# Forgetting attention and a bilinear feed-forward layer in one kernel: the last 64 queries as full tiles, value products as visits of their own, the last output in halves, and a new order

## The chip, the cores and the metric

The kernel runs on one core of a Trainium2 chip. The core has engines with a queue each, which run side by side and wait for one another through semaphores: TensorE (PE in the profile; its weight loads are PEld), VectorE (DVE), ScalarE (ACT), GpSimd (POOL) and SyncE (SP), which issues most of the DMA transfers. Every queue is worked off strictly in the order in which its instructions stand. The metric is the device time of one execution in microseconds (us).

## The reference, cut to what matters

There are 8 batches with 8 heads each, 576 positions and 64 dimensions per head. The attention has a decay from a running sum of log f; its output is the input of a bilinear layer.

```python
cum = np.cumsum(np.log(np.clip(f, 0.0001, 1.0)), axis=-1)
scores = scale * np.matmul(q, k.transpose(0, 1, 3, 2))
scores = np.where(causal, -1e9, scores + cum[:, :, :, None] - cum[:, :, None, :])
attn = exp(scores - max) / sum            # 576 x 576 per head
x = np.matmul(attn, v)                    # to 4608 tokens x 512
out = ((x @ w_a) * (x @ w_b)) @ w_out     # 512 -> 1536 -> 512
```

## The kernel before, in words

**Units of the attention.** A unit t is a pair of heads of one batch: t = 4 * batch + pair, 32 units in all. One head of the pair lies on partitions 0 to 63 of the tiles qT and kT, the other on partitions 64 to 127, so a score matmul contracts over 64 partitions only, and the matmuls of the two heads are issued one after the other for the two halves of the array. The 576 queries are four blocks of 128 (i = 0 to 3) and a last one of 64 (i = 4). `groups` (line 640) puts them in four groups: group 0 is the blocks 1 and 0, group 1 block 2, group 2 block 3, group 3 the last 64 queries. In group 3 the result of one head goes to partitions 0 to 63 and that of the other to 64 to 127, so its matmuls use 64 x 64 of the array each (`qk_group`, lines 413 to 429): two with 512 keys, two with 64 keys, and two that add the causal mask from `low` and `neg64`.

**What a unit goes through.** Score matmuls write a PSUM tile `sc`, of which there are two (RING, line 104); each group takes one. DVE adds the decay and takes the maximum (line 520 of `do_decay`), and writes S; that frees `sc`. ACT takes the exponential and its sum (551, and 547 for i = 4), DVE the reciprocal (561, 559), POOL multiplies by it (569). The blocks 0 to 2 make the tile PA, the blocks 3 and 4 the tile PB. SP issues a transposing DMA of each (`do_tr`, line 583; for batch 0 PE transposes instead). PE then multiplies with the values (`do_pv`, 611, and `do_pv4`, 627, for the last 64 queries), and DVE copies the result to xT (237 and 638).

**Visits of TensorE.** A scheduled piece of work is an `Op`; one for PE is called a visit here. For batches 0 and 1 (`EARLY`) the groups 0 and 1 are visits, and groups 2 and 3 are one. From batch 2 on (units 8 to 31, `MASKP`) there are two visits a unit: groups 0 and 1 together, and groups 2 and 3 together (line 693). The first of them also does the value products of unit t - 2 (LAG, line 656); their last 64 queries go to a spare corner of the group-0 tile of `sc`, so that tile is only free again when DVE has copied them out (`do_ev4`, 638).

**The feed-forward layer.** The 4608 tokens are cut into eleven chunks. For each of 12 feature blocks there are four matmuls for w_a (`psa`) and four for w_b (`psb`, line 888), ACT copies the first result, DVE multiplies the two (899); then three groups of four matmuls a block of 128 tokens make the output (`pso`, 908), which ACT and DVE copy out in turn (233, 237) and SP stores (918). A chunk can only start when all its tokens' attention is done. There are 372 such groups of four matmuls; they fill PE between the visits of the attention.

**The order.** All Ops are made in program order and numbered. A list of numbers, ORDER (line 990), then gives the order in which they are issued, and CHOICE (line 1092) says which engine an Op that could run on several takes. Nothing is scheduled on the chip: each engine runs its part of ORDER in that order. q, k and v of a batch come by SP's DMAs (244, 263), are cast to fp16 (235, 237) and q and k are transposed on PE (278); f comes by two DMAs (165); its running sum needs `clip`, a logarithm, `scan` and `low_part` (177 to 185). The weights come by POOL's DMAs (385), eight for w_a and w_b.

Of the kernel before, what the change touches and what calls it, by code (L numbers as in the profile page):

```python
# [25 lines left out]
def kernel(  # L26
# [11 lines left out]
    nc = tc.nc  # L38
# [23 lines left out]

    crow = perm.tile([128, S], FP16, tag="crow", name="crow")
# [25 lines left out]
    def paddings():  # L89
        for x in PB:  # L90
            nc.gpsimd.memset(x[:, 12, 64:128], 0.0)
        for i in range(2):
            nc.gpsimd.memset(nv[i][64:128, NSB - 1, :, :], 0.0)
# [12 lines left out]
            "sc": 2, "pv": 1, "ff": 3}  # L106
# [35 lines left out]
    def take(op, tag):  # L142

        users = [op]
        op.takes.append((tag, users))
        return users
# [257 lines left out]
    def qk_group(t, g):  # L404
# [6 lines left out]

        if g == 3:
# [232 lines left out]
    ev_ops, late, last_bc, last_pb = {}, {}, [], []  # L645
# [12 lines left out]
    def attention(t, base):  # L658
# [34 lines left out]
        for gs in ([(0,), (1,), (2, 3)] if b in EARLY else [(0, 1), (2, 3)]):  # L693
# [3 lines left out]
            old = None  # L697
            if gs == (0, 1) and (t - LAG) // NP not in EARLY and t >= LAG:
                old = t - LAG
# [8 lines left out]
            qk = Op("PE", dur * COLS * 1.06 + (0.08 if gs == (2, 3) else 0.0), stage, deps, prio=prio(gs[0]), mode="row", name=f"qk{t}.{gs[0]}")  # L708
            if old is not None:
                qk.durs = {"PE": dur * COLS * 1.06 + 0.1 + 10 * 128 * COLS * 1.05 + 0.15}  # L710
                qk.last = "col"
                qk.deps.extend(late[old][0])
            if qk_prev:
                qk.deps.append(qk_prev)
            qk_prev = qk
# [4 lines left out]
            if old is not None:  # L720
                late[old][1](qk, sc_of[0])
            for u in (kq_users[("q", b)], kq_users[("k", b)]):
                u.append(qk)
        direct_ex = {}
# [201 lines left out]
    def ffn(t0, n):  # L926
# [27 lines left out]
        for tb in range(n // 128):  # L954
            p = base + 12 + tb
            prev = []
            for part in range(3):
# [11 lines left out]
                prev = [mo]  # L969
            oc = Op(*(("DVE", 0.69) if tb % 2 else ("ACT", 0.59)), lambda e, tb=tb: ff_ocopy(e, t0, tb), prev, prio=-2000 + p, name="ocopy")  # L970
# [16 lines left out]
    for n in cuts:  # L987
# [3 lines left out]
        26 1 0 20 32 38 44 3 4 27 2 19 21 22 28 5 11 6 12 29 30 7 13 14 8 9 33 10 31 34 267 16 18 23-25 61 64  # L991
# [5 lines left out]
        235 108 236 249 85 250 95 90 127 1635-1637 1639 87 253 1641 128 1640 1638 133 1642 184 86 91 129 185 134  # L997
        130 1643 96 1644-1646 97 153 258 132 131 254 251 141 98 102 135 172 99 178 136 59 126 259 142 255 256
# [6 lines left out]
        342 1680 1681 343 1682 484 380 381 344 485 274 391 392 296 474 297 303 304 239 1683-1685 308 467 475  # L1005
        298-300 476 305 1686 324 486 1688 306 393 346 347 353 354 488 348 349 487 302 417 301 307 468 350 355
        1689 240 1690 1691 418 237 469 419 238 470 471 374 477 479 408 1693 1694 420 421 396 397 1695 1696
        411 412 356 403 1697-1700 352 337 395 351 330 394 480 357 338 310 1701 315 481 404 316 398 399 1702 483
        422 425 432 423 311 1703 426 400 1704 482 405 309 491 1687 493 360 358 1705 1706 427 433 406 312 439 440
        1707 1709 1711 435 1710 1708 1712 428 313 434 314 424 1713 442 1714 441 402 401 407 478 429 431 1715  # L1010
        1717 1718 446 447 1716 453 361 1719-1721 1723 454 443 533 448 1725 1722 449 1726 1727 496 345 494 1724
# [4 lines left out]
        547 554 414 532 531 461 462 556 1749 537 1751-1753 559 1754 1755 1757 1756 1759-1761 1758 560 1762 663  # L1016
        445 459 558 574 535 549 551 557 1763 1765 1764 542 1766 564 1767 1769 1768 1770 561 565 1771-1777 664
        543 544 658 550 1778 576 665 562 563 566-568 577 666 1779 1780 659 660 580 588 578 569 570 581 661 463
        1781 464 1783 465 1785 582 1784 1750 594 1782 587 1787 583 1788 590 1786 466 595 1789 1791 579 584 1790
        589 591 601 615 669 1745 670 592 571 572 667 683 674 1793 1795 1792 596 597 1794 598 1796 1797 602 1798  # L1020
        585 616 575 593 603 604 606 599 586 600 607 605 1799-1801 608 1802 671 609 618 610 1804-1806 619 622 630
        629 636 637 620 623 1807 624 672 632 673 611 612 668 684 675 1809 631 625 1810 639 638 681 613 614 725
        679 621 1811 1813-1815 643 1812 644 1817 617 640 633 1816 645 648 626 649 642 1819 1818 1820 646 647 627
        1821-1824 676 651 650 686 677 652 678 653 654 641 628 634 635 682 1825 1827 1829 690 1826 692 691 698
        704 1828 688 705 697 700 1831 1833 1830 693 706 1834 699 707 1835 1832 694 687 1836 701 689 856 656 655
        851 1803 1837-1839 711 708 712 1840 696 680 695 710 685 716 713 703 857 726 709 714 702 715 852 717
        1841-1843 1845 1844 1847 728 1849 1846 718 719 732 1848 720 1850 1851 1853 734 1854 722 721 730 739 733
        740 1852 1855 1856 746 747 1857 853 1858 1859 731 741 854 749 742 735 1860 858 748 859 860 729 855 863
        767 809 736 753 754 864 727 755 743 750 758 759 756 1862-1864 724 723 1808 1861 1867 770 1868 1869
        760 761 737 768 757 861 762 1865 745 763 764 774 788 776 790 751 738 752 789 791 792 782 772 775 781 794  # L1030
        744 1870 1872 1873 784 777 783 1874 1876 766 773 765 877 875 873 1877 1875 771 865 1878 866 867 1880
        1882 862 795 796 778 785 810 769 1879 800 797 801 1881 802-804 798 1883 786 793 780 799 787 779 805 806
# [107 lines left out]
```

## Time and profile before

| | us |
|---|---|
| median of 3 runs | 416.04 (415.64 to 416.44) |
| the profiled execution | 417.89 |
| its span, first to last instruction | 416.2 |
| PE busy | 390.6 (94%) |
| DVE / ACT / POOL busy | 302.3 / 278.1 / 255.0 |
| first matmul starts | 5.38 |
| mean granted TensorE clock | 0.995 |

The profile is of one execution, 1.85 us longer than the median of the runs shown. Busy times say how much of the span an engine worked; PE's ends are modelled, so two matmuls that run one behind the other overlap in these figures, and the distance from one start to the next is the better measure. A group's line gives its busy time, the mean duration of one instruction, then the idle time in front of it and what ended that. A timeline row gives start, time, engine and line, operation, tiles and shapes, the number of merged instructions, and in brackets the idle time in front.

### The profile page before, as it was taken

The numbers are of one execution on the slowest core, as the hardware profiler recorded it, in microseconds if no ns is written. First come the engines' busy times: TensorE is split into PE (matmuls) and PEld (weight loads), VectorE is DVE, ScalarE is ACT, GpSimd is POOL, SyncE is SP. The second block draws the span as 40 slices with busy tenths as digits, with TensorE's granted clock in tenths as the row PEclk, the third lists the DMA queues.
The fourth block names the chain that finished last, engine by engine and source line by source line (L and its number), as shares of the span: only waits on it lengthen the run. The fifth ranks groups of instructions, "written<-read, shape, count | busy, mean of one in ns | idle before, by whom it ended". The sixth has DMA issues, their size and how long they took to land. (4 is left out here: it accounts for less than half of the span.)

```text
span 416.2 us, 10946 instructions
## 1 busy us (share of the span) xinstructions
PE 390.6 (94%) x3860; PEld 212.1 (51%) x3860; DVE 302.3 (73%) x1006; ACT 278.1 (67%) x790; POOL 255.0 (61%) x439
## 2 busy tenths in 40 slices
PE   1789999799998999999999999999999999999996
PEld 1456766566655544444444544444454444444552
DVE  5998998697777778867877889688877885342240
ACT  5886997685777578786878778677787773231231
POOL 7999898469477867686685586766856655000000
PEclk9999999899999999999999999999999999999999
DMA  8999999999999999999999999999966738200202
GB/s 261 240 217 237 184 223 224 180 234 195 243 247 224 285 246 194 275 229 273 235 229 245 251 253 196 230 215 292 213 138 165 162 63 173 95 0 2 101 2 76
DMA packets 153432, 80.58 MB, mean 194 GB/s; under 512 B 130720, under 2 KB 133280, under 8 KB 153376
## 3 DMA queue, kind: packets, MB, share of 16 engines
q1 hardware_dynamic: 149616, 75.15, 79.3%
q0 software_dynamic: 3760, 4.72, 6.9%
q8 instruction: 30, 0.49, 0.5%
q14 instruction: 26, 0.21, 0.2%
HBM read 52.05 MB, written 9.58 MB: 148 GB/s over the span
## 5 line engine op out<-in xcount | busy, mean ns | idle before, releaser
L520 DVE CUSTOM_DVE_ANT_0 S<-sc,spread 64x576 f32<-64x576 f32 (+4 forms) x232 | 124.9, 562 | 10.6 <-ACT PA L551 3.1
L888 PE MATMUL psb<-xT,wb 128*128 128x512 f16 (+2 forms) x528 | 116.1, 343 | 0.4 <-ACT a L233 0.4
L888 PE MATMUL psa<-xT,wa 128*128 128x512 f16 (+2 forms) x528 | 115.8, 342 | 0.3
L899 DVE TENSOR_TENSOR ht<-psb,a 128x512 f16<-128x512 f32 (+2 forms) x132 | 77.4, 589 | 34.0 <-PE psb L888 30.6
L233 ACT CAST a<-psa 128x512 f16<-128x512 f32 (+2 forms) x132 | 66.2, 502 | 51.6 <-PE psa L888 43.5
L551 ACT ACTIVATE PA<-S,st 128x256 f16<-128x256 f32 (+2 forms) x168 | 84.1, 503 | 24.2 <-DVE st L520 22.6
L908 PE MATMUL pso<-wout,ht 128*128 128x512 f16 x432 | 98.5, 379 | 0.0
L569 POOL TENSOR_SCALAR PA<-PA,st 128x384 f16<-128x384 f16 (+2 forms) x192 | 89.8, 480 | 12.4 <-DVE st L561 11.0
L569 POOL TENSOR_SCALAR PB<-PB,st 128x512 f16<-128x512 f16 (+1 forms) x96 | 67.5, 712 | 30.1 <-DVE st L561 16.4
L888 PEld LDWEIGHTS <-wb 128*128 128x128 f16 x528 | 50.1, 98 | 41.3 <-issue 1.3
L888 PEld LDWEIGHTS <-wa 128*128 128x128 f16 x528 | 49.4, 98 | 40.8 <-issue 1.8
L908 PEld LDWEIGHTS <-ht 128*128 128x128 f16 x432 | 40.6, 98 | 46.7 <-issue 0.5
L551 ACT ACTIVATE PB<-S,st 128x512 f16<-128x512 f32 x56 | 40.1, 717 | 11.7 <-DVE st L520 7.7
L410 PE MATMUL sc<-kT,qT 64*128 64x256 f16 (+5 forms) x480 | 43.7, 277 | 3.3 <-ACT PA L551 1.5
L551 ACT ACTIVATION_READ_ACCUMULATOR PA<-S,st 128x1 f32 x168 | 31.9, 190 | 0.0
L561 DVE RECIPROCAL st<-st 128x2 f32<-128x2 f32 x128 | 18.5, 158 | 18.2 <-ACT PB L551 13.1
L410 PEld LDWEIGHTS <-qT 64*128 64x128 f16 (+1 forms) x480 | 17.0, 98 | 28.2 <-issue 18.5
L486 POOL TENSOR_SCALAR_AFFINE_SELECT spread<-spread 128x256 f32<-128x256 f32 x24 | 9.8, 408 | 35.1 <-DVE st L520 35.1
L237 DVE CAST xT<-pv 128x512 f16<-128x512 f32 (+1 forms) x40 | 23.0, 575 | 8.8 <-PE pv L611 8.6
L547 ACT ACTIVATE PB<-S,st 128x576 f16<-128x576 f32 x28 | 21.8, 777 | 9.9 <-issue 6.5
L233 ACT COPY osb<-pso 128x512 f32<-128x512 f32 x19 | 10.9, 575 | 24.3 <-DMA out_dram<-osb 12.8
L520 DVE CUSTOM_DVE_ANT_1 S<-sc,spread 128x256 f32<-128x256 f32 x48 | 19.6, 420 | 9.4 <-PE sc L627 4.7
(85 smaller groups left out, 427.6 us busy)
## 6 DMA issues: line engine op xcount, KB each, us to landing
spread<-cum_d SPq DMA_DIRECT2D x24, 576.0 KB, 5.6
out_dram<-osb SPq DMA_DIRECT2D x36, 256.0 KB, 3.0
q<-in_q_dram SPq DMA_DIRECT2D x15, 576.0 KB, 5.7
k<-in_k_dram SPq DMA_DIRECT2D x15, 576.0 KB, 5.5
v<-in_v_dram SPq DMA_DIRECT2D x32, 256.0 KB, 5.5
wout<-in_moe_w_out_dram POOLq DMA_DIRECT2D x3, 512.0 KB, 6.4
v<-in_v_dram SPq DMA_DIRECT2D x8, 128.0 KB, 4.9
wa<-in_moe_w_a_dram POOLq DMA_DIRECT2D x2, 512.0 KB, 8.6
```

Of the source, the lines that this page charges most:

```text
L233: nc.scalar.copy(out=out_, in_=in_)
L237: VEC[e].tensor_copy(out=out_, in_=in_)
L410: nc.tensor.matmul(out=dst, lhsT=lhsT, rhs=rhs, start=start, stop=stop, skip_group_check=True)
L486: nc.gpsimd.affine_select(out=x, in_=x, compare_op=mybir.AluOpType.is_ge, fill=NEGBIG, base=0, pattern=[[0, 2], [-1, 128]], channel_multip ...
L520: nc.vector.tensor_tensor_reduce(out=o, in0=x, in1=y, scale=-1.0, scalar=3e38, op0=ADD, op1=MIN, accum_out=m)
L547: nc.scalar.activation(out=p_blocks(t, 4), in_=T[("s" if direct else "z", t, 4)], func=EXP, bias=st[:, 8:9], scale=sign, accum_out=st[:, 1 ...
L551: nc.scalar.activation(out=p_blocks(t, i)[:, :, h, :], in_=(T[("s", t, i)][:, h, :] if direct else T[("z", t, i)][:, h * n:h * n + n]).rea ...
L561: nc.vector.reciprocal(out=st[:, 20 + 2 * i:22 + 2 * i], in_=st[:, 10 + 2 * i:12 + 2 * i])
L569: VEC[e].tensor_scalar(out=p, in0=p, scalar1=st[:, c:c + 1], scalar2=1.0, op0=MUL, op1=MUL)
L888: nc.tensor.matmul(out=p[:, 0:n], lhsT=w16[:, db, 128 * fb:128 * fb + 128], rhs=xTflat[db][:, t0:t0 + n], start=(db == 0), stop=(db == 3))
L899: nc.vector.tensor_tensor(out=ht[:, 0:n], in0=T.pop(("psb", t0, fb))[:, 0:n], in1=T.pop(("a16", t0, fb))[:, 0:n], op=MUL)
L908: nc.tensor.matmul(out=o, lhsT=T[("ht", t0, fb)][:, 128 * tb:128 * tb + 128], rhs=wout16[:, fb, :], start=(fb == 0), stop=(fb == 11))
```

## The change

Four things are changed.

1. From batch 2 on the scores of the last 64 queries (group 3) are made with 128 x 128 matmuls. POOL copies the two heads' 64 queries into a tile `qd` (two of them, zero elsewhere) whose two diagonal blocks are the two heads, so that one matmul gives both; three matmuls (512 keys, 64 keys, mask with the block-diagonal tile `lowd`) take the place of six. `paddings` clears `qd` and `lowd` at the start and fills `lowd`.
2. The visits of units 8 to 31 are one a group instead of one for two groups, and the value products of unit t - 2 are a visit of their own, `pv`, which may come any time after group 0 of unit t.
3. The last 128 tokens' output is copied in two halves, by DVE and ACT, and stored by two DMAs, from ACT's queue and SP's.
4. ORDER and CHOICE are replaced as a whole by another result of the search.

What the new order does can be read from the sequence of instructions on each engine. On PE the groups of a unit come as 0, 1, 3, 2 as a rule, and group 0 of unit t + 1 mostly stands right behind group 2 of unit t. SP issues the two loads of f ahead of the first loads of q and k; before, q came first. DVE casts the first q and k alone (before: q by DVE and ACT, k by POOL) and makes both low parts of the first 256 positions; POOL makes both of the rest, the first of them ahead of the second q's casts. Two of the w_b loads (512 KB each) stand on POOL behind the normalizations of block 2 and some of block 3 of batch 0. SP issues the first transpose of unit 5 ahead of its second one, of unit 6's second one and of two loads of the running sum. The 372 groups of feed-forward matmuls keep their own order.

```diff
+    qd = [perm.tile([128, 128], FP16, tag=f"qd{i}", name=f"qd{i}") for i in range(2)]
+    lowd = perm.tile([128, 128], FP16, tag="lowd", name="lowd")
...
     def paddings():
+        for x in (*qd, lowd):
+            nc.gpsimd.memset(x, 0.0)
+        for r in HP:
+            nc.gpsimd.tensor_copy(out=lowd[r, r], in_=low[0][r, 0:64])
...
+        if g == 3 and t in MASKP:
+            x = qd[t % 2]
+            mm(c[:, 0, :], x, kT[:, pr, 0:SF], start=True, stop=True)
+            mm(c[:, 1, 0:64], x, kT[:, pr, SF:S], start=True)
+            mm(c[:, 1, 0:64], lowd, neg64, stop=True)
+            T[("s", t, 4)] = c.rearrange("p a k -> p (a k)")[:, 0:S]
+            return
...
+    def last_queries(t):
+        b, pr = divmod(t, NP)
+        for r in HP:
+            nc.gpsimd.tensor_copy(out=qd[t % 2][r, r], in_=T[("T", "q", b)][r, pr, SF:S])
...
-        for gs in ([(0,), (1,), (2, 3)] if b in EARLY else [(0, 1), (2, 3)]):
+        for gs in ([(0,), (1,), (2, 3)] if b in EARLY else [(0,), (1,), (2,), (3,)]):
...
-            def stage(_, gs=gs, old=old):
+            def stage(_, gs=gs):
                 for g in gs:
                     qk_group(t, g)
-                if old is not None:
-                    do_pv(old, (0, 1, 2, 3), {"A", "B"})
-                    do_pv4(old, T.pop(("spare", t)))
...
+            if full:
+                cp = Op("POOL", 0.4, lambda _: last_queries(t), [kq_ops[("q", b, pr)], o_p] + last_qd[-1:], prio=prio(0),
+                        name=f"qd{t}")
...
+            old = t - LAG
+            if gs == (0,) and b not in EARLY and old // NP not in EARLY:
+                pv = Op("PE", 10 * 128 * COLS * 1.05 + 0.15,
+                        lambda _, old=old: (do_pv(old, (0, 1, 2, 3), {"A", "B"}), do_pv4(old, T.pop(("spare", t)))),
+                        [qk, *late[old][0]], prio=prio(0), mode="col", name=f"pv{old}")
+                sc_of[0].append(pv)
+                late[old][1](pv, sc_of[0])
...
+    def last_copy(e, t0, tb, part):
+        if ("osb", t0, tb) not in T:
+            T[("osb", t0, tb)] = osb_pool.tile([128, 512], FP32, tag="osb", name="osb")
+        c = slice(256 * part, 256 * part + 256)
+        cast(e, T[("osb", t0, tb)][:, c], T[("pso", t0, tb)][:, c], False)
+
+    def last_store(t0, tb, part):
+        r0, c = t0 + 128 * tb, slice(256 * part, 256 * part + 256)
+        (nc.sync if part else nc.scalar).dma_start(out=out[r0:r0 + 128, c], in_=T[("osb", t0, tb)][:, c])
...
+            if t0 + 128 * tb + 128 == NT:
+                ou = None
+                for part, (e, d) in enumerate((("DVE", 0.41), ("ACT", 0.39))):
...
     ORDER = """
-        26 1 0 20 32 38 44 3 4 27 2 19 21 22 28 5 11 6 12 29 30 7 13 14 8 9 33 10 31 34 267 16 18 23-25 61 64
...
+        0 1 26 20 32 38 3-6 27 28 11 7 2 29 30 12 21 22 8 10 9 13 14 19 33 34 23 24 31 25 18 61 64 35 70 106 15
...
     CHOICE = """
-        PDPPPPAADAADPDADAPDAPPPDDDDDAADDDDDDDDADAAADAADDDDDAAAAAAADADAAAADAAAAADDAAAAAAAAAAAAAADDAAAADAAADDA AAA
+        DDPPDDAADDADAPDAPPDDPPPDDAADDDADDDDADDAAAAAADADDADDDDAAAAADADAAAAAAAADADDADAAAAAAADAADADADAAAADADAAA AAA
```

More of the change, by code (lines that the diff above doesn't have):

```diff
@@ L105 @@
             "LA0": 1, "LA1": 1, "LA2": 1, "LA3": 1, "PA": 4, "PB": 2, "PTA": 3, "PTB": 2, "st": 6, "ht": 14, "a16": 3, "osb": 2,
-            "sc": 2, "pv": 1, "ff": 3}
+            "sc": 2, "qd": 2, "pv": 1, "ff": 3}
     SM = 3 * 128
@@ L644 @@
     MAXD = {0: 0.42, 1: 0.69, 2: 0.96, 3: 1.22, 4: 0.75}
-    ev_ops, late, last_bc, last_pb = {}, {}, [], []
+    ev_ops, late, last_bc, last_pb, last_qd = {}, {}, [], [], []
     first_of = {}
@@ L696, in attention @@
                       + (128 * len(groups[g]) * (t not in MASKP) if g < 3 else 128) for g in gs)
-            old = None
-            if gs == (0, 1) and (t - LAG) // NP not in EARLY and t >= LAG:
-                old = t - LAG
-            def stage(_, gs=gs, old=old):
+            full = gs == (3,)
+            def stage(_, gs=gs):
                 for g in gs:
                     qk_group(t, g)
-                if old is not None:
-                    do_pv(old, (0, 1, 2, 3), {"A", "B"})
-                    do_pv4(old, T.pop(("spare", t)))
[L708 to L713, printed above, removed]
+            qk = Op("PE", (640 * COLS if full else dur * COLS * 1.06) + (0.08 if gs == (2, 3) else 0.0), stage, deps,
+                    prio=prio(gs[0]), mode="full" if full else "row", name=f"qk{t}.{gs[0]}")
+            if full:
+                cp = Op("POOL", 0.4, lambda _: last_queries(t), [kq_ops[("q", b, pr)], o_p] + last_qd[-1:], prio=prio(0),
+                        name=f"qd{t}")
+                last_qd.append(cp)
+                kq_users[("q", b)].append(cp)
+                take(cp, "qd").append(qk)
+                qk.deps.append(cp)
+            elif qk_prev:
                 qk.deps.append(qk_prev)
+            elif b not in EARLY and (t - 1, 3) in qk_ops:
+                qk.prev.extend([qk_ops[(t - 1, 2)], qk_ops[(t - 1, 3)]])
             qk_prev = qk
@@ L719, in attention @@
                 in_turn(qk, f"qk{g}", t)
-            if old is not None:
-                late[old][1](qk, sc_of[0])
             for u in (kq_users[("q", b)], kq_users[("k", b)]):
                 u.append(qk)
+            old = t - LAG
[5 more added lines that the diff above has]
+                late[old][1](pv, sc_of[0])
         direct_ex = {}
@@ L969, in ffn @@
                 prev = [mo]
+            if t0 + 128 * tb + 128 == NT:
+                ou = None
+                for part, (e, d) in enumerate((("DVE", 0.41), ("ACT", 0.39))):
+                    oc = Op(e, d, lambda e, tb=tb, part=part: last_copy(e, t0, tb, part), prev, prio=-2000 + p, name=f"ocopy{part}")
+                    uo.append(oc)
+                    ou = ou or take(oc, "osb")
+                    so = Op("SP" if part else "ACT", 0.53, lambda _, tb=tb, part=part: last_store(t0, tb, part), [oc],
+                            prio=-500 + p, land=packets(128, 1024))
+                    ou.extend([oc, so])
+                continue
             oc = Op(*(("DVE", 0.69) if tb % 2 else ("ACT", 0.59)), lambda e, tb=tb: ff_ocopy(e, t0, tb), prev, prio=-2000 + p, name="ocopy")
@@ new lines @@
+        1969-1971 798 895 896 816 897 797 1972 787 788 811 794 821 822 1973 823 1974 838 1976 1978 892 836 791
+        826 827 846 847 818 1975 1977 824 828-830 907 898 903 953 848 854 856 1979 849 1980 842 839 1982 812 806
+        831 819 813 908 820 832 825 853 855 841 860 917 1983 1981 844 867 861 857 1984 1985 868 837 1986 840 850
+        852 899 904 858 1987-1989 863 834 833 1990 1992 843 910 1994 869 954 905 1991 862 1996 1993 918 926 872
[5 rows of a table added]
+        986 955 980 987 982 1000 984 990 991 1100 992 993 951 952 2023 2018 1002 2026 2029-2031 1003 1006 2034
@@ new lines @@
+        975 988 2032 1102 983 1010 1005 989 1108 1109 976 994 996 977 1055 1011 1024 1025 1017 2027 1012 2036
+        2038 1013 2035 1026 1019 1018 968 2037 1027 1020 2039 969 1008 2040 1007 1031 1028 1032 2041-2043 1033
[9 rows of a table added]
+        1176-1178 1180 1181 1169 1182 1188 1310 1189 1184 1191 1183 1158 1185 1159 1134 2093 2094 1172 2095 1190
+        1195 1196 1192 2097 1303-1305 1168 1160 1171 2098 1313 2091 1255 1197 1165 1140 1186 1200 2099 2100 1201
+        1193 1116 1202-1204 1206 2102 2104 1212 1216 2106 2103 1220 1228 1198 1199 2108 2107 2110 1222 1221 1223
@@ new lines @@
+        2233 1587 1590 2234 1588 1589 1608 1598 1592 1615 1578 1554 1559 2235 2236 1605 1610 2238-2240 1616 1609
[3 rows of a table added]
+        1656 1655 2261 1607 1689 1599 1619 1625 1626 2262-2264 1638 2266 1634 1635 2265 1661 1662 2268 2267 1657
[4 rows of a table added]
+        1674 1673 2291 2292 1723 1721 1724 2293 2296-2298 2301 1675 2294 1676 2295 2290 2299 2302 1725 2303 1726
+        1677 1678 2304 2305 2300 2306-2308 2310 2309 2311 2312 2314 2316 2313 2315 2317-2320 1727 2322 2321
+        2323 2324 2326 2325 2327 2328 1728 2330 2329 2331 2332 2334 2336 2333 2335 2338 2340 2337 2339 2341 2342
```

78 lines of the change are left out of this document (16 added, 62 removed), and 110 rows, old and new, of the table ORDER.

## The prediction

> **What bounds the kernel now.** I read the page's busy times first.
>
> ```profile
> PE 390.6 (94%) x3860; PEld 212.1 (51%) x3860; DVE 302.3 (73%) x1006; ACT 278.1 (67%) x790; POOL 255.0 (61%) x439
> ```
>
> PE is the bound, so the change gains only by PE time saved or PE waits removed. The table by stretches (length, then PE, PEld, DVE, ACT, POOL busy, clock, DMA share, GB/s) says where waits are:
>
> ```profile
> 10.40:20.80 10.40, 8.00 (x107) 5.13 (x108) 9.71 (x22) 9.33 (x36) 10.00 (x17) 1.00 0.93 240
> 52.00:62.40 10.40, 10.40 (x145) 7.04 (x144) 10.17 (x42) 10.02 (x33) 9.39 (x17) 1.00 1.16 223
> 72.80:83.20 10.40, 7.53 (x81) 5.49 (x76) 7.06 (x30) 6.80 (x24) 4.96 (x7) 0.87 1.11 180
> 145.00:340.00 195.00, 194.32 (x1840) 94.46 (x1840) 156.72 (x555) 146.11 (x415) 132.04 (x219) 1.00 0.95 219
> ```
>
> There are three stages. To 62 us DVE, ACT and POOL are full, and a late start stays late. From 62 to about 141 us all engines have gaps and DMA is full. From 145 us PE is full and the others have 38 us or more to spare. The hole of the second stage, in the timelines of SP and PE:
>
> ```profile
> 71.90 5.21 SPq L583 DMA_TRANSPOSE PTB<-PB  x1
> 77.21 1.76 SPq L583 DMA_TRANSPOSE xT<-PA  x1
> ```
>
> ```profile
> 77.47 0.60 PE L888 MATMUL psb<-xT,wb 128*128 128x256 f16 x4
> 77.91 0.60 PE L888 MATMUL psa<-xT,wa 128*128 128x256 f16 x4
> 80.99 0.53 PE L611 MATMUL pv<-xT,nv 128*64 128x128 f16 x6 [2.49 <-DMA xT<-PA]
> 81.46 1.03 PE L888 MATMUL psb<-xT,wb 128*128 128x256 f16 x4
> ```
>
> SP stands 5.21 us in one transpose (unit 5's second), the first one of the same unit behind it goes out at 77.21, and its value products wait 2.49 us. The same FFN group then takes 1.03 instead of 0.60 until 84 us, since the clock has dropped (0.87 and 0.96 in the two slices).
>
> **The change part by part.** I make the sum against the profiled execution, 417.89 us (span 416.2 and 1.7 around it). It is 1.85 above the median; I assume the same for both kernels and take the sum off the median.
>
> *Modes of the array, -1.5.* The chain of waits has FFN groups of four at equal steps, except behind an attention visit:
>
> ```profile
> 285.03 0.97 PE psa L888 x4
> 286.00 0.86 PE psb L888 x4
> 286.86 0.86 PE psa L888 x4
> ```
>
> So a change of tile shape costs 0.10 (starts to starts: 98 ns, all kinds alike). In instruction order there are 248 such changes before and 233 after, since groups 2 and 0 of neighbouring units now stand together and the full tiles have the FFN's shape: -15 x 0.1.
>
> *Full tiles, +0.6.* PE's timeline has the old matmuls of the last queries, and the nearest full-array matmuls of 128 columns:
>
> ```profile
> 76.59 0.43 PE L410 MATMUL sc<-kT,qT 64*64 64x512 f16 x4
> 76.86 0.20 PE L410 MATMUL sc<-crow,pick 64*64 64x64 f16 x2
> ```
>
> ```profile
> 28.75 0.53 PE L589 MATMUL psP<-ident,PA 128*128 128x128 f16 x6
> ```
>
> Two 512-column and two 64-column matmuls, one of each for either head, start within 0.27: the heads run side by side. With the mask pair a visit is 0.30 in mode, 24 times. The full one is 0.216 (a quarter of 0.86) and two short ones; six of 128 columns above, less one matmul's 0.22, are 0.06 apart: 0.33 in all. That is 24 x 0.03 = +0.6 with rounding. Bounds: short ones at half (27 ns, as they have 64 columns) -0.7; both weight loads of 98 ns (mean of the PEld groups) uncovered, +2.7. I take 0.06 as the row of the same shape and full array.
>
> [...]
>
> *POOL's copies, 0.* 24 x 2 copies of 64x64; POOL's 32x32 copies take 0.20 and its 64x64 selects 0.23, so +10 us. They are needed one visit ahead, and POOL has 195 - 132 = 63 us idle in the stage where most lie; with the cover gone, each visit of group 3 waits up to 0.46, 24 x 0.46 = 11. The clearing adds 0.9 to POOL before 8 us, where it waits 1.27 for k.
>
> *Start, +2.2.* SP issues f ahead of q:
>
> ```profile
> 0.81 0.45 SPq L263 DMA_DIRECT2D q<-in_q_dram  x1
> 1.32 1.63 SPq L165 DMA_DIRECT2D cum_f<-in_f_dram  x2
> 4.83 0.49 DVE L235 TENSOR_SCALAR q<-q 128x512 f16<-128x512 f32 x1 [2.57 <-DMA q<-in_q_dram]
> 11.89 1.02 DVE L494 TENSOR_REDUCE st<-sc 128x2 f32<-128x512 f32 x2
> ```
>
> q is used 4.02 after its issue. f's issues move q to 0.81 + 1.68 = 2.49, in DVE at 6.51. DVE now has alone, by durations of before: q 0.49 + 0.60, clip 0.64, scans 1.66, k 0.49 + 0.88, high part 1.27, low parts 0.84, a copy 0.76, 7.63 in all: first maximum at 14.1 instead of 11.89. Bounds: 0 (clip and scans done while q is under way and the rest of the stage's work spread better) and +3.2 (POOL's low part too, which waits for the high one and stands ahead of the second q's casts). I take +2.2. POOL's two w_b loads go out at about 40 instead of 30.5 and 17.9 us; such loads land 8.4 to 10.9 after issue, and PE needs them some 9.2 later: 0 to +1.7, taken as 0, inside +3.2.
>
> *The transpose, -4.0.* Unit 5's first transpose goes past its second one, unit 6's second and two loads of the running sum, so past 5.21 of issue, and its value products come 2.6 us of PE work later. The wait goes (2.5), and 1.5 of slow clock behind it: from 81.46 to 83.97 three groups start 0.84 apart instead of the 0.44 of 77.47 to 77.91, 1.2, and the value products ahead of them lose the rest. Behind it are late next: the second transposes of units 5 and 6, by the 1.8 that the first one takes. The q load of batch 3's second half likewise goes ahead of unit 9's transposes; its wait of 1.38 at 129.15 may go, which I leave in the range. Bounds: 0 and -6.
>
> *Own visits, +1.0.* From 145 to 340 us PE now loses some 3.5 in all by its starts. After it, group 3 stands 0.86 us of PE work behind the value products at units 8, 11, 15, 19 and 20; the `sc` in between must be freed by the copy of the last 64 values (0.2 on DVE), sometimes behind a decay (0.49). Group 0 stands 2.0 to 2.5 behind group 3 at nine units and needs two decays of 0.75. These nearly fit; a tenth here and there over 14 places gives 1.0 (bounds -1, as decays come more evenly, and +6).
>
> *End, -0.3.* The last copy:
>
> ```profile
> 412.32 0.59 ACT L233 COPY osb<-pso 128x512 f32<-128x512 f32 x1 [4.64 <-PE pso L908]
> ```
>
> Halves of 256 columns take about 0.4 (DVE's 256-column forms 0.38), so -0.2, a second queue -0.1; bounds -0.5 and +0.4 (ACT's issue behind its own copy).
>
> Sum: -1.5 + 0.6 + 2.2 - 4.0 + 1.0 - 0.3 = -2.0; 416.04 - 2.0 = 414.0; a profiled execution like before's would be 415.9.
>
> **The rivals.**
>
> A, slower: the stall comes back later. Unit 8's value products come 13.5 us of PE work behind its group 2 (before 16.5, and it still waited 1.00 at 106.84), unit 10's 13.2 (before 15.6). If DMA, at a share above 1 here, delivers no sooner, they wait 3.0 and up to 2.4 longer; at 4.0 together the transpose's gain is gone: 416.0 + 2.0 = 418.0 (at 5.4, 419.4). It decides from 2.0 in all. For: DMA is full and SP issues without pause. Against: the reordering adds nothing to SP's issues, so what unit 5 gains need not be lost twice.
>
> B, slower: the tight visits. If two pieces of DVE work stand ahead, 0.49 + 0.75 - 0.86 = 0.4 is missing at each of 14 visits: 5.6 instead of 1.0, 418.6; from 0.21 each it is slower. For: only two `sc`. Against: DVE is idle for 38 of 195 us.
>
> C: the start's delay is hidden, since PE after 62 us follows DMA: 414.0 - 2.2 = 411.8. For: the gaps there. Against: the three engines are full until 62.
>
> D: only the wait goes and the slow clock's 1.5 comes back at another wait: -0.5, 415.5. For: the clock fell after one wait of 2.5 and waits of 0.7 to 1.4 remain (106.84, 129.15, 140.58). Against: none of these has a clock below full behind it.
>
> E: both short matmuls of a full tile wait for their weight load: 0.216 + 2 x 0.098 = 0.41, 24 x 0.11 = +2.7 instead of +0.6: +0.1, 416.1. For: the loads' row of 98 ns. Against: the 0.06. [...]
>
> **How the numbers follow.** A measurement tells 0.2% (0.8 us) from no change. Forecast 0.40 (its own range 412.4 to 415.6: the start and the steady stage moved by half their bounds), C 0.13, D 0.06, E 0.05, A 0.22, B 0.14. Faster (forecast and C) 0.53, same (D and E) 0.11, slower (A and B) 0.36. The range takes in C with the full tiles at their lower bound (411.8 - 1.3 = 410.5) and B (418.6), with little beyond it: 419.0.
>
> **What would show it.** Right: 15 changes of shape less, each 0.1; visits of group 3 at 0.33; the first maximum near 14.1; no wait and no slow group at 81 us; waits under 5 us from 145 to 340. Wrong: a wait at the products of unit 8 or 10 of 3 or more; waits in front of groups 3 and 0 that end with DVE's S or copies; POOL's copies as releasers of PE; a last matmul before 409 us in its profile with a start like before's (C).

## The result and the profile after

The changed kernel takes 415.33 us (median of 22 runs), the kernel before 416.56 in the same runs; the ratio is 0.9951 (95% interval 0.9931 to 0.9972), so 2.0 us less by the ratio and 1.2 by the medians. 414.0 was forecast, in a range of 410.5 to 419.0. The profiled execution took 413.75 us with a span of 412.0. It lies 1.6 us under its kernel's median, and the profiled execution of before 1.3 over the median of these runs, so the 4.1 us between the two profiles are twice what the change is worth; a second profile of the kernel before (below) was needed to read them. Two profiled executions among the experiments were disturbed (spans of 647 and 771 us); of those two runs only the other times are used.

The page's busy times, changed kernel:

```profile
PE 388.2 (94%) x3788; PEld 209.6 (51%) x3788; DVE 302.8 (73%) x1011; ACT 277.8 (67%) x788; POOL 265.1 (64%) x490
```

POOL has its 10 us more, PE 72 matmuls and 2.4 us less than in the first profile of the kernel before; against its second profile (389.2 us busy, no slow clock) it is 1.0. The table by stretches (columns as shown of before):

```profile
10.40:20.80 10.40, 7.37 (x103) 4.68 (x102) 9.57 (x19) 9.11 (x29) 8.94 (x15) 1.00 0.92 201
72.80:83.20 10.40, 9.87 (x143) 7.46 (x143) 9.50 (x37) 8.20 (x27) 8.35 (x15) 1.00 1.04 222
145.00:340.00 195.00, 192.63 (x1770) 93.31 (x1769) 156.92 (x559) 147.40 (x418) 141.60 (x257) 1.00 0.94 217
```

The start is a little emptier, the hole at 73 to 83 us is filled, and the steady stage now has 2.4 us in which PE is not busy, where it had 0.7.

PE's timeline around the last 64 queries of a unit. An FFN group of four starts right behind the three full matmuls:

```profile
284.50 1.02 PE L914 MATMUL psa<-xT,wa 128*128 128x512 f16 x4
285.36 0.41 PE L417 MATMUL sc<-kT,qd 128*128 128x512 f16 x2
285.60 0.19 PE L417 MATMUL sc<-neg,lowd 128*128 128x64 f16 x1
285.63 1.03 PE L914 MATMUL psb<-xT,wb 128*128 128x512 f16 x4
```

From 285.36 to 285.63 is 0.27 us for the visit, and the group in front of it takes its 0.86, so there is no change of shape on either side.

The start, in the timelines of SP and DVE, and four of PE's larger waits (us in total, times, longest):

```profile
0.81 1.65 SPq L172 DMA_DIRECT2D cum_f<-in_f_dram  x2
2.51 0.45 SPq L270 DMA_DIRECT2D q<-in_q_dram  x1
6.28 1.33 DVE L242 TENSOR_SCALAR q<-q 128x512 f16<-128x512 f32 x2 [1.32 <-DMA q<-in_q_dram]
12.86 1.01 DVE L514 TENSOR_REDUCE st<-sc 128x2 f32<-128x512 f32 x2
```

```profile
PE psT L285 <- DVE q L242: 7.3, 2, 6.9
PE pv L631 <- DMA xT<-PA: 1.4, 3, 0.8
PE pv L631 <- DMA PTA<-PA: 1.1, 1, 1.1
PE psa L914 <- ACT a L240: 0.8, 1, 0.8
```

Since the 1488 FFN matmuls keep their sequence, the start of a given one is a ruler for all kernels here. These are starts in us, from the traces, for four kernels and a second execution of the kernel before:

```
FFN matmul number            0    150    200    300    500    700   1000   1487
before                    33.0   74.5   86.3  109.1  156.7  214.3  298.4  411.9
before, second execution  33.2   74.5   83.0  105.8  153.8  211.5  295.4  408.8
changed                   34.2   76.9   85.5  107.6  153.0  211.0  294.4  407.5
changed, 64 x 64 tiles    34.8   78.1   86.8  108.7  154.4  213.1  298.2  411.7
```

Against the second execution of before the changed kernel is 2.4 us late at matmul 150, 0.8 early at 500 and 1.3 early at the end. Nearly all of its gain lies between 77 and 153 us, where DMA is full (a share of 1.08 in the changed kernel's profile, 1.13 in the first one of before): from matmul 200 to 500 it takes 67.5 us, before 70.4 and 70.9. This gain is the order's and not the full tiles': the five traces of kernels with the new order there (one with 64 x 64 tiles, some with the start or one store put elsewhere) have 66.7 to 67.8 us, the six in the old order, with and without full tiles, 69.4 to 71.1. From matmul 500 to the end the tiles decide: the new order takes 257.3 us with 64 x 64 tiles and 254.5 to 256.1 in the five traces with full ones, before 255.2 and 255.0.

### The profile page after: what moved, and what is told of

Its sections match the earlier page's. It is cut to its first block, busy times and chain, and to the rows that moved or that the text cites. A ratio compares the mean times of both kernels' runs of the same rounds, so it can differ in the third digit from the quotient of the medians.

```text
span 412.0 us, 10863 instructions
## 1 busy us (share of the span) xinstructions
PE 388.2 (94%) x3788; PEld 209.6 (51%) x3788; DVE 302.8 (73%) x1011; ACT 277.8 (67%) x788; POOL 265.1 (64%) x490
## 5 line engine op out<-in xcount | busy, mean ns | idle before, releaser
L540 DVE CUSTOM_DVE_ANT_0 S<-sc,spread 64x576 f32<-64x576 f32 (+4 forms) x232 | 126.4, 562 | 13.3 <-PE sc L417 6.1
L925 DVE TENSOR_TENSOR ht<-psb,a 128x512 f16<-128x512 f32 (+2 forms) x132 | 77.4, 590 | 34.2 <-PE psb L914 26.3
L589 POOL TENSOR_SCALAR PA<-PA,st 128x256 f16<-128x256 f16 (+2 forms) x192 | 90.3, 480 | 18.3 <-DVE st L581 12.3
L934 PE MATMUL pso<-wout,ht 128*128 128x512 f16 x432 | 100.0, 380 | 0.0
L589 POOL TENSOR_SCALAR PB<-PB,st 128x512 f16<-128x512 f16 (+1 forms) x96 | 67.6, 712 | 24.3 <-DVE st L581 13.1
L914 PEld LDWEIGHTS <-wb 128*128 128x128 f16 x528 | 49.1, 98 | 40.2 <-issue 1.8
L417 PE MATMUL sc<-kT,qT 64*128 64x128 f16 (+4 forms) x384 | 35.8, 274 | 3.1 <-ACT kT L240 1.4
L240 ACT COPY osb<-pso 128x512 f32<-128x512 f32 (+1 forms) x19 | 10.8, 569 | 32.3 <-DMA out_dram<-osb 15.7
L244 DVE COPY osb<-pso 128x512 f32<-128x512 f32 (+1 forms) x18 | 12.1, 674 | 20.8 <-PE pso L934 14.9
L631 PEld LDWEIGHTS <-nv 128*64 128x64 f16 x640 | 19.5, 110 | 13.1 <-issue 9.8
L417 PEld LDWEIGHTS <-qT 64*128 64x128 f16 (+1 forms) x384 | 13.8, 96 | 23.0 <-issue 15.6
```

The costliest lines, as they stand in the source:

```text
L240: nc.scalar.copy(out=out_, in_=in_)
L244: VEC[e].tensor_copy(out=out_, in_=in_)
L417: nc.tensor.matmul(out=dst, lhsT=lhsT, rhs=rhs, start=start, stop=stop, skip_group_check=True)
L540: nc.vector.tensor_tensor_reduce(out=o, in0=x, in1=y, scale=-1.0, scalar=3e38, op0=ADD, op1=MIN, accum_out=m)
L589: VEC[e].tensor_scalar(out=p, in0=p, scalar1=st[:, c:c + 1], scalar2=1.0, op0=MUL, op1=MUL)
L631: nc.tensor.matmul(out=o[HP[h], 128 * i:128 * i + 128], lhsT=vt[:, j, pr + NP * h, :], rhs=pt[:, base_blk[i] + 2 * block_at(t, i, j) + h, ...
```

## The experiments

All times are medians, and all ratios stand against the kernel before measured beside it, whose medians were 416.5 to 416.6 each time. The changed kernel has 415.2 over both of its runs. Starts of matmuls and waits are those of one execution of each kernel, and two executions of the same kernel can differ by 3 us, as the next part shows.

### Each kernel once more

Expected of the changed kernel:

> The changed kernel once more, unaltered, to see which waits of its first trace come back and to have it on the same chip as the three runs beside it. By my theory: 0.995 of the kernel before (-2.0 us), first matmul at 6.9 us, no wait of 1 us or more on PE between 62 and 145 us, and the waits at 153 to 172 us (0.6, 0.7 and 1.1 us) again. If the first trace was a chance draw (it was 1.6 us under this kernel's median), PE loses 1 to 2 us more somewhere, most likely in 62 to 172 us, where DMA is full.

Measured: 415.24 us, ratio 0.9983 (0.9947 to 1.0019). The interval takes in both no change and the first ratio; the median is within 0.1 of the first run's, 1.2 us under before, while by this ratio the change is worth 0.7 us.

Expected of the kernel before:

> The kernel before once more, unaltered, for a second trace. By my theory the wait of 2.5 us at 81 us with the slow clock behind it comes back (11 to 12 us of waits on PE from 62 to 145 us). If the first trace, 1.3 to 1.85 us above the median, was a chance draw, these waits are 1 to 2 us smaller here.

Measured: one execution, 414.82 us (span 413.1). Its PE timeline where the first trace had a wait of 2.49 us and FFN groups of 1.03:

```profile
77.92 0.60 PE L888 MATMUL psa<-xT,wa 128*128 128x256 f16 x4
79.06 0.36 PE L611 MATMUL pv<-xT,nv 128*64 128x128 f16 x6 [0.54 <-DMA xT<-PA]
79.35 0.61 PE L888 MATMUL psb<-xT,wb 128*128 128x256 f16 x4
```

The wait is 0.54 and the groups behind it start 0.44 apart. By the starts of PE's matmuls (what lies between two of them beyond the usual distance of such a pair) the waits from 62 to 145 us are 8.7 us here and 11.8 in the first trace; the other stages are equal to within 0.2. So 3 us of what the prediction read from one profile belong to that execution and not to the kernel.

### The transposes

Unit 5's first transpose ahead of its second one, in the kernel before:

```diff
-        ... 1687 493 360 358 1705 ...
+        ... 1687 493 358 360 1705 ...
```

> The kernel before with one exchange on SP's queue: unit 5's first transpose ahead of its second one. If the place on the queue was what cost 4.0 us, its transpose goes out at 71.9 instead of 77.2 us, the wait of 2.5 us in front of unit 5's value products and the slow clock behind it are gone, and the kernel is 0.990 of the kernel before (-4.0 us). If only the wait goes and the slow clock comes back at another wait: -2.5 us (0.994). If DMA delivers the following transposes later by as much (rival A): within 0.2%, with longer waits at the products of units 6 to 8.

Measured: 417.32 us, ratio 1.0021 (0.9986 to 1.0055), if anything slower. SP's and PE's timelines:

```profile
73.82 1.23 SPq L583 DMA_TRANSPOSE xT<-PA  x1
75.14 4.58 SPq L583 DMA_TRANSPOSE PTB<-PB  x1
79.81 0.54 SPq L473 DMA_DIRECT2D spread<-cum_d  x1
```

```profile
94.65 0.25 PE L611 MATMUL pv<-xT,nv 128*64 128x128 f16 x2 [1.41 <-DMA xT<-PA]
```

The wait at 81 us is gone, and others pay: these products wait 1.4 us, which they did in neither execution of before (there the next ones waited, 0.7 and 0.9). Over 62 to 145 us the waits are 10.4 us, more than the 8.7 of the second execution. This is rival A's case in small: from 62 to 145 us DMA has a share of 1.15 in the kernel before, and one transfer ahead put another back.

The reverse in the changed kernel, unit 5's first transpose behind its second one again:

```diff
-        358 1781 491 ...
+        1781 491 ...
-        ... 1819 536 360 402 ...
+        ... 1819 536 360 358 402 ...
```

> The changed kernel with unit 5's first transpose behind its second one on SP's queue, as in the kernel before. If the place on the queue is worth 4.0 us, it is 4 us slower, with a wait near 81 us in front of unit 5's value products. By the run that moved it in the kernel before (0.8 us slower there, other waits took the place): the wait comes at that place, the others behind it shrink, and the time is within 1 us of the changed kernel.

Measured: 416.80 us, 1.6 us over the changed kernel (ratio to before 1.0009, 0.9982 to 1.0037). The wait comes, but not at 81 us and not at unit 5's products:

```profile
98.80 0.36 PE L631 MATMUL pv<-xT,nv 128*64 128x128 f16 x6 [2.56 <-DMA xT<-PA]
```

So by the medians this place is worth 1.6 us in the new order and nothing in the old one. How sure that is: the interval here lies above that of the changed kernel's first run (0.9931 to 0.9972) but overlaps that of its second. In the trace the kernel is already 1.7 us late at FFN matmul 100 (63.9 against 62.3), ahead of the exchange; from number 200 to 500 it takes 70.4 us, as long as in the old order, and the kernel before with the exchange alone takes 71.0. The exchange pays only together with the rest of the new order.

### The full tiles

64 x 64 matmuls again, in the changed kernel's visits:

```diff
-        if g == 3 and t in MASKP:
+        if False:
             x = qd[t % 2]
```

> The changed kernel with the scores of the last 64 queries by six 64 x 64 matmuls again, in the same visits; POOL's copies to the two tiles remain but nobody reads them. By the trace of the changed kernel a full visit is 0.27 us with no change of shape beside the FFN; with tiles it is 0.30 and two changes of 0.10 at most places (some 40 more changes in all): 24 x 0.03 + 4 = 4 to 5 us slower than the changed kernel. By the sum of the prediction the matmuls themselves differ by less than 1 us and only the changes of shape count: 3 to 4 us slower. If full tiles bring nothing (weight loads uncovered, rival E): within 0.2% of the changed kernel or faster.

Measured: 417.83 us, 2.6 us over the changed kernel and 1.3 over the kernel before (ratio 1.0031, 1.0000 to 1.0061, so the latter is at the edge of what can be told). The interval lies wholly above that of the changed kernel's first run, 0.9931 to 0.9972. A visit in its PE timeline:

```profile
288.09 1.02 PE L914 MATMUL psa<-xT,wa 128*128 128x512 f16 x4
289.05 0.43 PE L417 MATMUL sc<-kT,qT 64*64 64x512 f16 x4
289.32 0.20 PE L417 MATMUL sc<-neg,low 64*64 64x64 f16 x2
289.44 1.04 PE L914 MATMUL psb<-xT,wb 128*128 128x512 f16 x4
```

The group in front takes 0.96 and the visit 0.39, together 0.22 more than with full tiles (0.86 and 0.27). Over the 24 visits, each by its own neighbours, that is 4.4 us on PE, of which 2.6 show in the median. In the two traces, the six visits between FFN matmuls 150 and 500 cost 0.1 to 0.2 us (76.3 against 76.1) and the 18 behind them 2.8. The program has 273 changes of shape, before has 248, the changed kernel 233. So the own visits cost 25 changes, and the new order with 64 x 64 tiles in it is no better than the old one.

Full tiles alone, in the kernel before (visits and order kept; POOL's copies issued with the unit's first visit; tiles cleared at the start):

```diff
     def paddings():
+        for x in (*qd, lowd):
+            nc.gpsimd.memset(x, 0.0)
+        ...
             def stage(_, gs=gs, old=old):
+                if gs == (0, 1) and t in MASKP:
+                    for r in HP:
+                        nc.gpsimd.tensor_copy(out=qd[t % 2][r, r], in_=T[("T", "q", b)][r, pr, SF:S])
```

> The kernel before with the full tiles alone: POOL's two copies are issued with the unit's first visit, the last 64 queries take three full matmuls, visits and order stay. By the traces a tiled visit takes 0.397 us with its change of shape to the FFN, a full one 0.273 and one change less, so 24 x 0.126 = 3.0 us are saved: 0.993 of the kernel before. By the prediction's terms (-1.5 for the changes of shape, +0.6 for the tiles) it is -0.9. If the copies on POOL are late (they stand behind the normalizations), PE waits in front of group 3 and the gain is eaten.

Measured: 416.78 us, ratio 0.9996 (0.9963 to 1.0030): nothing. It has the same 233 changes of shape as the changed kernel. The visits are cheaper by 1.9 us in all, not by the 3.0 expected: from its start to the next matmul's a visit took 0.397 us before, and takes 0.284 at 15 places, but 0.380 at the other nine, where a change of shape stays behind it. Against these 1.9 us, the trace has two waits that the kernel before has not, 2.8 us together, one for a weight load behind POOL's clearings and one for POOL's copy:

```profile
35.37 0.60 PE L904 MATMUL psa<-xT,wa 128*128 128x256 f16 x4 [1.57 <-DMA wa<-in_moe_w_a_dram]
167.68 0.42 PE L416 MATMUL sc<-kT,qd 128*128 128x512 f16 x2 [1.24 <-POOL qd L717]
```

The second attempt clears the tiles with unit 5's first visit and issues the copies a visit earlier:

```diff
+                if (t, gs[0]) == (5, 0):
+                    clear_qd()
+                n = t + 1 if gs == (2, 3) and pr < NP - 1 else t if gs == (0, 1) and pr == 0 else None
+                if n in MASKP:
+                    for r in HP:
+                        nc.gpsimd.tensor_copy(out=qd[n % 2][r, r], in_=T[("T", "q", b)][r, n % NP, SF:S])
```

> The kernel before with the full tiles alone, as in the run on that, but without the two new waits that its trace shows: the tiles are cleared with unit 5's first visit (there they were cleared ahead of the w_a loads, and PE waited 1.6 us for w_a at 35 us), and POOL's copies are issued a visit earlier (there one of them was 1.3 us late at 168 us). If the full tiles' 3.0 us were only covered by these two waits, PE's waits are again those of the kernel before and it is 2 to 3 us faster than before (0.993 to 0.995). If they are hidden where DMA sets the pace (8 of the 24 units lie before 145 us), about 2 us of them remain, 0.995. If POOL's copies cost elsewhere, it stays within 0.2% of before, with PE waits that end with POOL.

Measured: 416.71 us, ratio 0.9984 (0.9952 to 1.0016), nothing again, though the wait for POOL's copy is gone and that for w_a is 0.4. The chain of waits of this run and PE's timeline show one place where the saving is lost:

```profile
270.51 6.48 DMA q<-in_q_dram
277.07 1.16 POOL q L243
```

```profile
278.28 0.44 PE L286 MATMUL psT<-ident,q 64*128 64x64 f16 x18 [1.07 <-POOL q L243]
```

The chain of the first profile of the kernel before has the same load in it (269.94, 6.09 us), with PE arriving just as the cast is done; that of its second profile has not. The last run moves this one load on SP's queue, ahead of two transposes and an output store:

```diff
-        ... 1295 2062 2063 1238 1237
-        2060 1438 2064 ...
+        ... 1295 2062 2063 1438 1238 1237
+        2060 2064 ...
```

> The second run on full tiles alone, with one load moved: batch 7's first q (issued near 270.5 us there) goes ahead of unit 23's two transposes and an output store on SP's queue, so out at 261 to 265 us. In the run without this move PE waits 1.1 us at 278 us for POOL's cast of this q, which waits for the load, and its chain of waits runs through that load. If the full tiles bring nothing in the old order because each saving ends at such a load, this wait shrinks to under 0.3 us and the FFN matmuls from number 1100 on come 0.8 to 1.1 us earlier against number 700 than in the run without the move (112.6 us there); the median falls by about 1 us, to 415.5 to 416. If PE's own work is the limit there, the matmuls keep their distance and another wait takes the place.

Measured: 414.94 us, ratio 0.9950 (0.9920 to 0.9979). SP and PE:

```profile
259.33 0.37 SPq L271 DMA_DIRECT2D q<-in_q_dram  x1
```

```profile
271.72 2.32 PE L929 MATMUL pso<-wout,ht 128*128 128x512 f16 x10
273.97 0.44 PE L286 MATMUL psT<-ident,q 64*128 64x64 f16 x18
```

There is no wait in front of the transposes any more, and FFN matmul 1100 comes 111.3 us behind number 700 (322.9 - 211.6) instead of 112.6 (327.0 - 214.4). With one load moved, the full tiles in the old order reach the ratio of the whole change. What this proves of the load is less. The intervals of the second attempt and this run overlap. The two kernels issue the same work up to about 259 us, and yet numbers 0 to 700 take 178.7 us here and 180.3 there, so much of the distance between the two traces is chance. The first attempt, where PE waited 0.2 us at this place, has 111.4 us from 700 to 1100 (326.2 - 214.8) without the move. And no run moves the load without the full tiles. So the wait of 1.07 us is gone with the load moved, but that this load was what kept the full tiles from paying is not shown.

### The start and the end

The first 50 pieces of work as in the kernel before, all others as in the changed kernel:

```diff
-        0 1 26 20 32 38 3-6 27 28 11 7 2 29 30 ...
+        26 1 0 20 32 38 44 3 4 27 2 19 21 22 28 5 11 6 12 29 30 ...
```

> The changed kernel with the first 50 pieces of work in the order and on the engines of the kernel before (q ahead of f; q by DVE and ACT, k by POOL), all later ones in the new order. If the new start costs what its trace shows (first matmul 1.5 us later, 2.0 us more of PE's waits up to 62 us), this is 2 to 3.5 us faster than the changed kernel in the same call, with the first matmul near 5.4 and the first maximum near 11.9 us. If the delay is hidden behind the transfers that follow (rival C), within 0.2% of the changed kernel, with as much more waiting between 62 and 145 us.

Measured: 415.14 us, ratio 0.9974 (0.9944 to 1.0004), level with the changed kernel's 415.24 measured beside it.

The same with the last output copied whole and stored by SP:

```diff
     def last_copy(e, t0, tb, part):
+        if part == 0:
+            return
...
-        c = slice(256 * part, 256 * part + 256)
+        c = slice(0, 512)
```

> The changed kernel with the start of the kernel before (first 50 pieces of work, as in the run on the start) and the last output copied whole by ACT and stored by SP. The halves run one after the other in the changed kernel (0.42 and 0.37 against 0.59 whole), so the end is 0.2 us shorter. By the run on the start, which came out level with the changed kernel, the trace shows PE's waits up to 62 us smaller by 2 us or more and those from 62 us on larger by as much (the start's delay is hidden): 414.5 to 415 us, 0.2 to 0.5 under the changed kernel. If the start is worth 2 us after all: 413.

Measured: 416.08 us (412.64 to 417.52), ratio 0.9969 (0.9938 to 1.0000), so not told apart from the changed kernel. Its trace shows how the start is lost: FFN matmul 0 is 1.0 us earlier than in the changed kernel (33.2 against 34.2), number 300 1.3, number 500 0.8, number 700 0.7 and number 1000 not at all (294.3 against 294.4). So the start's delay is made up, as rival C has it, but in this trace between 211 and 294 us, where PE is full (busy for 83.0 of these 83 us in the changed kernel's profile), and not from 62 to 145 us, where rival C puts it. (The trace is of an execution of 413.52 us, 2.6 under its kernel's median.) The end gained nothing: from the last matmul's start to the end of the span are 4.5 us in the changed kernel, 4.6 here and 4.3 in both profiles of the kernel before. The halves run one behind the other. The timeline of the changed kernel's end has DVE's half as the releaser of ACT's:

```profile
407.94 0.42 DVE L244 COPY osb<-pso 128x256 f32<-128x256 f32 x1 [1.56 <-PE pso L934]
408.40 0.37 ACT L240 COPY osb<-pso 128x256 f32<-128x256 f32 x1 [5.05 <-DVE osb L244]
408.80 0.33 SPq L950 DMA_DIRECT2D out_dram<-osb  x1
```

### The waits of the new order

The largest wait of the changed kernel's middle that has a plain cause on SP's queue is at 153 us: ACT waits for an output store before it can copy the next output, and PE waits for ACT.

```profile
152.38 0.59 ACT L240 COPY osb<-pso 128x512 f32<-128x512 f32 x1 [2.60 <-DMA out_dram<-osb]
153.01 1.02 PE L914 MATMUL psa<-xT,wa 128*128 128x512 f16 x4 [0.42 <-ACT osb L240]
```

The store was moved ahead of a transpose and a load of v:

```diff
-        ... 803 741 742 1962 ...
+        ... 803 741 1955 742 1962 ...
-        ... 786 891 1955 835 ...
+        ... 786 891 835 ...
```

> The changed kernel with one output store moved on SP's queue, ahead of unit 12's second transpose and a load of v (it goes out near 144.7 instead of 148.6 us). In the changed kernel ACT waits 2.6 us for its landing at 152.4 us, PE 0.6 us behind it at 153.0 and 0.7 at 155.0. If the place on SP's queue is the cause, both waits go and FFN matmuls from 157 us on are 1.0 to 1.3 us earlier than their distance from the start before: 0.997 of the changed kernel. If the next transfer is what then comes late (as it was with unit 5's transposes), the wait at 172 us grows by as much and the time is within 0.2% of the changed kernel.

Measured: 414.93 us, ratio 0.9948 (0.9919 to 0.9977), 0.3 under the changed kernel, too little to be told from no change. The waits at 153 and 155 us are gone; FFN matmul 500 comes 75.8 us behind number 150 (152.5 - 76.7) instead of 76.1, number 700 134.4 instead of 134.1. The wait at 172 us has grown from 1.05 to 1.4, and one of 0.84 stands at 201 us.

Everything together, start, end and store:

> The store's move together with the start of the kernel before and the whole last copy, the version meant to beat both. Start 1.0 us earlier at 60 us, the waits at 153 to 155 us gone (1.3 to 1.8), the end 0.2: if they add up, 2.5 us under the changed kernel, 0.991 of the kernel before. If each early gain comes back as a later wait for a transfer, as the start did in the run with the whole last copy (1.0 us ahead at 61 us, 0.1 at 267 us), it is within 0.2% of the changed kernel.

Measured: 413.73 us (median of 12 runs), ratio 0.9945 (0.9915 to 0.9975). By its ratio it is not told apart from the changed kernel or the one with the store alone, by its median it is the fastest of all here, 2.8 us under before. In its trace FFN matmul 150 comes as late as in the changed kernel (76.8 and 76.9) although number 0 was 1.1 ahead, and the wait at 172 us has become 1.65:

```profile
171.28 0.36 PE L631 MATMUL pv<-PTA,nv 128*64 128x128 f16 x6 [1.65 <-DMA PTA<-PA]
```

## Why the prediction was right, and where it was not

The direction and size came out, and two of its terms were far off in ways that cancelled.

- **Modes and full tiles, -0.9 forecast, -2.2 by the same sum with the measured visit.** The 233 changes of shape at 0.10 are as said. The term of the tiles was mis-sized: +0.6 was taken from 128-column matmuls 0.06 apart, but the two short ones have 64 columns and start 0.028 to 0.029 us apart, so a visit is 0.27 instead of 0.33, the lower bound of -0.7. Rival E fell: it has 0.41 for a visit, and in the 0.27 no weight load shows.
- **Start, +2.2 forecast.** FFN matmul 100 starts at 62.3 us, in the two traces of before at 60.0 and 60.2, so the size came out. The path did not: the first maximum comes at 12.86 us, 1.0 late and not 2.2, and the first 50 pieces of work make 1.1 of the delay (61.2 with the old start). These 1.1 are made up later, from 211 us on in one trace and between 61 and 77 us in another (that of everything together). The rest was not taken apart.
- **The transpose, -4.0 forecast.** This step failed in its cause. The wait at 81 us was 0.54 to 2.49 us in five executions of kernels with the old order there, and the clock fell behind two of them (0.87 and 0.85 in a slice), so a term of 4.0 was read from one unlucky execution. The exchange alone gains nothing in the old order and, by the medians, is worth 1.6 us in the new one, through a wait at 99 us and not at 81. The stage gained all the same: from FFN matmul 200 to 500 the changed kernel takes 67.5 us, before 70.4 and 70.9. The full tiles make none of it (67.6 with 64 x 64 tiles). The exchange is needed for it, by the one trace without it (70.4), but is not enough (71.0 in the old order); which of the other moves it needs beside it stays open.
- **Own visits, +1.0 forecast.** PE's waits from 145 to 340 us are 5.8 us against 3.5 to 3.7 before, so +2.1, in one trace of the changed kernel (the prediction's sign for being right was under 5). The cause was another one: not the copies of values or two decays at tight visits (rival B), but an output store at 153, the transposes of k behind it at 155, and a transposing DMA at 172 (0.6, 0.7 and 1.1 us by the starts). The 25 changes of shape that the own visits add were inside the count of 233, and it took the run with tiles to see that the order pays for them only with full tiles.
- **POOL's copies, 0.** They release no wait in the changed kernel's list. In the first run on full tiles in the old order they cost 1.2 us at one visit, and the clearing put a weight load back by 1.6.
- **End, -0.3 forecast.** The traces have +0.2 (4.5 us behind the last matmul's start against 4.3). ACT's half waits for DVE's, which the prediction had side by side; but the whole copy in the new order has 4.6, so the 0.2 have another cause, which was not found. The 0.1 for a second queue was the author's estimate; no run shows it by itself.

Of the other rivals, A and D do not show in the changed kernel's trace: no value product waits more than 1.1 us, and the clock is 1.00 in the stretches shown.

That the sum of -2.0 meets what was measured (1.2 by the medians, 2.0 and 0.7 by the two ratios) is thus partly luck: the tiles were off by 1.3 us and the transpose by 2.4 or more, in opposite directions.

## What to carry to other kernels

A saving on the engine that is busy nearly all the time (PE, 94% of the span) is not yet a saving of time: in the old order full tiles took 1.9 us off PE's visits, and two attempts gained nothing, with new waits of 2.8 us in the one and of 1.5 us (0.4 and 1.07) and a fallen clock in the other. A third attempt, with one load earlier on its queue, reached the gain of the whole change. So look which wait the engine meets next before you count its savings, and change the order together with the work. And where DMA is full (a share of 1.10 to 1.15 from 62 to 145 us here), take a second profile before you price a wait from the first one; moving one transfer ahead there alone (unit 5's transpose in the old order) only moved the wait.

## What the runs showed of the hardware that was not expected

PE's granted clock fell behind two of five waits of 1.75 to 2.56 us. These are the waits, at about 81 us where nothing else is said, and what the next FFN groups of 256 columns took from start to start (0.44 at a clock of 1.00):

```
kernel                         wait, us   groups behind it
before                         2.49       0.82 to 0.86 for 2.5 us, at once
full tiles, second attempt     2.04       0.44 twice, then 0.7 and 0.85
full tiles, load moved         2.22       0.44
full tiles, first attempt      1.75       0.44
transpose back (at 98.8 us)    2.56       0.44
```

Here are the rows of the second attempt, from PE's timeline:

```profile
81.58 0.36 PE L626 MATMUL pv<-xT,nv 128*64 128x128 f16 x6 [2.04 <-DMA xT<-PA]
81.87 0.61 PE L909 MATMUL psb<-xT,wb 128*128 128x256 f16 x4
82.31 0.60 PE L909 MATMUL psa<-xT,wa 128*128 128x256 f16 x4
82.75 0.93 PE L909 MATMUL psb<-xT,wb 128*128 128x256 f16 x4
83.47 1.06 PE L909 MATMUL psa<-xT,wa 128*128 128x256 f16 x4
```

The slow groups begin 1.2 us after the wait has ended. The granted clock of the profile agrees: 0.87 from 72.8 to 83.2 us in the kernel before and 0.85 from 83.2 to 93.6 us here, against 1.00 from 72.8 to 83.2 us in the run with the load moved and from 93.6 to 104 us in the one with the transpose back. A wait of 2.56 kept the clock and one of 2.04 lost it, so in these runs the length alone doesn't decide. What does decide was not found out.
